# Attention, gated MoE and token/channel mixer on one core: Strassen weight tiles built piece by piece from plain float32 blocks, and second-layer operand sums on VectorE

## The chip, the cores and the metric

One core of a Trainium2 chip runs the whole program. The metric is the device time of one launch in microseconds (us). Five engines take part: PE (TensorE, matrix products), DVE (VectorE), ACT (ScalarE), POOL (GpSimd) and SP (SyncE), which issues every DMA of this kernel in the order in which the DMAs were written to its queue.

## The reference

Three stages follow one another (batch 4, 448 tokens, model width 768).

```python
# attention: 12 heads of 64, q and k normalised first
attn = softmax(scale * rmsnorm(q, g_q) @ rmsnorm(k, g_k).T) @ v
x = attn.transpose(0, 2, 1, 3).reshape(B, S, 768)
# gated unit
h = relu(x @ w_in); u, v = h[..., :512], h[..., 512:]
v_s = w_spatial @ layernorm(v) + b_spatial        # over tokens
x = (u * v_s) @ w_out
# mixer
u = x + (relu(x.T @ w_tok1) @ w_tok2).T           # over tokens
out = u + relu(u @ w_ch1) @ w_ch2                 # over channels, 768 -> 1536 -> 768
```

The weights `w_in`, `w_out`, `w_tok*` and `w_ch*` arrive as 64-bit floats.

## The kernel before, in words

**Planner.** The program is written as generators that yield between small steps. `merge` interleaves several generators; every instruction goes into a `Plan`, which estimates its cost (`estimate`), schedules all of them by a list scheduler (`place`) and then issues each engine's instructions in the planned order. All compute instructions are issued from one line (L418), so rows of the profile are told apart by tile names. An engine works its queue strictly in order, SP too.

**Number format.** Float32 products run as three passes over operands that are split in two parts: `HI` (rounded, written by ACT) and `LO` (the rest, a subtraction on DVE or POOL). `convert` turns 64-bit weights into float32 words: one ACT operation (Abs), two DVE `TENSOR_SCALAR` and two DVE `SCALAR_TENSOR_TENSOR`.

**Stages in time.** Attention runs in 24 slots (`Attention.slot`), two heads each; beside it run the preparation of weights and the gated unit (`moe`) of the first three batches. Then the last batch's `moe` runs beside the first token products. Then come the token products of all batches (`tokens`: tiles `h1ps`, `u_ps`, `tp<-x`), then the first channel layer `up` (tile `h2ps`), then the second one `down` (tile `o_ps`).

**Strassen.** Both channel layers use a Strassen-Winograd scheme with seven products of half-size blocks, in the order A11, A12, S2, S3, S1, S4, A22 (`PRODUCTS`). Each product has an operand made from the data (`operand`, from in-place sums in `sums`) and a weight tile of 128 x 2 x 2304 (HI and LO). The weight of a product is a block (B11, B21, B22) or a combination of blocks (T1 = B12 - B11, T2 = B22 - T1, T3 = B22 - B12, T4 = T2 - B21). A product of `up` is 12 groups of 9 matmuls; one of `down` is 7 groups of 18 matmuls. Weight tiles share two buffers (tag `w`), so the tile of a product can be written only after the product two places before it has ended. Operands have two buffers in `up` and three in `down`.

**Where the weight tiles come from.** All seven of each layer are made ahead of use, split and stored to scratch in device memory (`c1_d`, `c2_d`), and `fetch` reads one back (three DMAs of 768 KB) when its product comes up. The first layer's seven are made during attention by `blocks` (tiles `half`, `part`; 9 rounds of 4 conversions, 4 differences on POOL and 7 splits of 256 columns). Of the second layer, B11 and B21 are made by `plain` beside the last `moe` (tile `part`, 24 conversions and splits of 192 columns), and the other five by `mixed` beside `tokens` and `up` (tiles `s`, `half`, `h`, `part`; 12 conversions and 30 splits of 384 columns).

**Sums of the second layer.** In `down`, the sums for S2 and S3 (two each per slice of 128 columns, 28 in all, rows `c<-c,c 128x768`) run on POOL, in place.

## Time and profile before

| | us |
|---|---|
| median of 3 runs | 960.1 (959.32 to 965.97) |
| the profiled execution | 958.78 |
| its span, first to last instruction | 957.0 |
| PE / DVE / ACT / POOL busy in the span | 888.3 / 694.3 / 542.8 / 507.9 |
| attention with three `moe` | 0 to 480 |
| last `moe` and first token products | 480 to 572 |
| `tokens` | 572 to 650 |
| `up` | 650 to 801 |
| `down` | 801 to 957 |

The stage borders are read from the timeline to within a few us. A busy PE is not PE at its peak, since matmuls are pipelined and the ends of their rows are modelled; how much work a stage holds is read from counts and from stretches in which matmuls of one kind follow one another closely.

### The profile page before, as it was taken

How to read it: one execution, taken by the hardware profiler on the slowest of the kernel's cores; microseconds unless marked ns; L12 is line 12 of the kernel's file. 1: busy time of each engine (PE TensorE's matmuls, PEld its weight loads, DVE VectorE, ACT ScalarE, POOL GpSimd, SP SyncE). 2: the span in 40 equal slices, each digit the busy share in tenths (PEclk: the TensorE clock that was granted, in tenths of full speed). 3: DMA queues.
4: the chain of work that ended last, by engine and by line, in shares of the span. 5: the costliest groups of instructions: out<-in, count | busy, mean ns of one | idle time of the engine just before them, and what ended most of it. 6: DMA issues, size and time to landing. Idle time of an engine off the chain costs nothing.

```text
span 957.0 us, 16041 instructions
## 1 busy us (share of the span) xinstructions
PE 888.3 (93%) x5134; PEld 722.5 (76%) x5134; DVE 694.3 (73%) x1364; ACT 542.8 (57%) x1312; POOL 507.9 (53%) x609
## 2 busy tenths in 40 slices
PE   3888899999998989989989988989999999999998
PEld 1434467677565767657868987879998899999998
DVE  4888889886899787997636744784798754576753
ACT  5998978777767776775635533545423443322221
POOL 2465654786367675566723811465633208984340
PEclk9998999999999999998989999998999999999999
DMA  6655645567746667655588577963787673352461
GB/s 149 162 152 159 175 132 150 157 189 222 222 113 205 200 201 232 200 160 177 184 282 260 207 225 250 330 216 101 248 276 259 241 252 114 133 183 99 148 216 66
DMA packets 166245, 182.99 MB, mean 191 GB/s; under 512 B 77329, under 2 KB 138577, under 8 KB 164625
## 3 DMA queue, kind: packets, MB, share of 16 engines
q1 hardware_dynamic: 166160, 181.96, 60.9%
q8 instruction: 41, 0.67, 0.3%
q14 instruction: 44, 0.35, 0.1%
HBM read 124.24 MB, written 57.67 MB: 190 GB/s over the span
## 4 chain that ended last, share of the span: by engine, by line
PE 44%; DVE 7%; DMA 6%; ACT 3%; issue 3%; POOL 1%; SPq 0%; ACTq 0%; POOLq 0%; DVEq 0%
PE o_ps L418 16%; PE h2ps L418 14%; DMA c_d<-part 4%; PE xps L418 2%; PE u_ps L418 2%; PE tp L418 2%; PE ups L418 2%; PE vps L418 2%; DVE part L418 1%; DVE half L418 1%; PE av L418 1%; PE h1ps L418 1%; PE sps L418 1%; DMA x_d<-xo 1%; DMA x<-x_d 1%
## 5 line engine op out<-in xcount | busy, mean ns | idle before, releaser
L418 PE MATMUL h2ps<-op,w 128*128 128x448 f32 x756 | 157.7, 370 | 4.6 <-DVE x L418 3.3
L418 PEld LDWEIGHTS h2ps<-op,w 128*128 128x128 f32 x756 | 142.9, 190 | 17.7 <-DVE x L418 3.6
L418 PE MATMUL o_ps<-w,op 128*128 128x384 f32 x882 | 153.1, 334 | 0.0
L418 PEld LDWEIGHTS o_ps<-w,op 128*128 128x128 f32 x882 | 152.9, 188 | 0.0
L418 ACT ACTIVATE e<-sc,nm 112x448 f32<-112x448 f32 x192 | 120.5, 637 | 27.2 <-DVE nm L418 14.9
L418 DVE TENSOR_REDUCE nm<-sc 112x1 f32<-112x448 f32 x192 | 110.4, 614 | 13.1 <-PE sc L418 12.4
L418 PE MATMUL tp<-ident,e 112*128 112x112 f32 x672 | 94.3, 264 | 9.3 <-ACT e L418 3.1
L418 PEld LDWEIGHTS tp<-ident,e 112*128 112x128 f32 x672 | 73.1, 142 | 36.1 <-ACT et L418 4.7
L418 ACT ACTIVATE op<-c 128x768 fp32r<-128x768 f32 x49 | 41.6, 848 | 102.7 <-PE o_ps L418 101.4
L418 POOL TENSOR_SCALAR e<-e,sums 112x448 f32<-112x448 f32 x112 | 78.1, 710 | 17.2 <-DVE sums L418 12.7
L418 DVE TENSOR_TENSOR op<-c,op 128x768 fp32r<-128x768 f32 x49 | 68.8, 1405 | 22.7 <-ACT op L418 22.7
L418 PE MATMUL ups<-xp,wu 128*128 128x448 f32 x288 | 71.7, 385 | 5.3 <-ACT e L418 3.2
L418 DVE TENSOR_TENSOR c<-c,h2ps 128x448 f32<-128x448 f32 x84 | 50.6, 617 | 32.9 <-PE h2ps L418 32.8
L418 ACT ACTIVATE et<-tp 128x448 f32<-128x448 f32 x120 | 64.8, 548 | 16.4 <-PE tp L418 14.6
L418 POOL TENSOR_TENSOR c<-c,c 128x768 f32<-128x768 f32 x28 | 58.7, 2119 | 26.1 <-ACT c L418 23.1
L418 PE MATMUL xps<-wo,g 128*128 128x256 f32 x432 | 64.4, 299 | 6.4 <-ACT xo L418 6.2
L418 PE MATMUL av<-et,v 128*64 128x448 f32 x288 | 67.3, 557 | 0.5 <-ACT tg L418 0.5
L418 PEld LDWEIGHTS xps<-wo,g 128*128 128x128 f32 x432 | 57.3, 199 | 11.4 <-ACT xo L418 6.9
L418 PEld LDWEIGHTS ups<-xp,wu 128*128 128x128 f32 x288 | 52.5, 192 | 13.3 <-ACT e L418 3.6
L418 DVE TENSOR_TENSOR part<-half,part 128x256 fp32r<-128x256 f32 (+1 forms) x78 | 45.2, 582 | 18.1 <-ACT part L418 17.9
L418 POOL TENSOR_TENSOR u<-u,o 128x384 f32<-128x384 f32 x28 | 34.7, 1249 | 43.6 <-DVE o L418 30.4
L418 PE MATMUL vps<-wv,xp 128*128 128x512 f32 x216 | 56.9, 408 | 0.0
(136 smaller groups left out, 1797.4 us busy)
## 6 DMA issues: line engine op xcount, KB each, us to landing
w<-c_d SPq DMA_DIRECT2D x42, 768.0 KB, 6.6
c_d<-part SPq DMA_DIRECT2D x63, 256.0 KB, 2.9
wu<-wu_d SPq DMA_DIRECT2D x16, 768.0 KB, 5.2
wo<-wo_d SPq DMA_DIRECT2D x12, 1024.0 KB, 5.3
c_d<-part SPq DMA_DIRECT2D x30, 384.0 KB, 3.1
raw<-in_moe_w_ch_dram SPq DMA_DIRECT2D x36, 256.0 KB, 3.0
raw<-in_q_dram SPq DMA_DIRECT2D x48, 112.0 KB, 3.1
u<-u_d SPq DMA_DIRECT2D x28, 192.0 KB, 4.2
```

Of the source, the lines that this page charges most:

```text
L418: getattr(getattr(self.nc, op.engine), fn)(*args, **kwargs)
```

## The change

Scratch now holds plain float32 blocks without the split: B11, B12, B21, B22 of both layers, and later T1 and T2. Making a block is a conversion and a store alone (`whole`). B11 and B21 of the first layer are converted during attention (18 pieces of 256 columns), its B12 and B22 beside the last `moe` (18 more), and all four of the second layer beside `tokens` and `up` (24 pieces of 384 columns).

`fetch` is replaced by `build`: when a weight tile is due, its 2304 columns are made in six pieces of 384. A piece fetches one to three blocks (tile `src`, six buffers, 192 KB each), takes differences on POOL, splits on ACT and DVE (tile `w`), and for T2 stores T1 and T2 back to scratch. So each of the 14 tiles costs 6 ACT copies and 6 DVE subtractions shortly before its product, and each layer 24 POOL subtractions.

The sums of `down` run on DVE in place of POOL; those of `up` stay on POOL. In the planner the assumed cost of a DMA with long rows changes, and the slot windows of the merged generators change. `divisors` takes its tile from another pool.

```diff
-        return max(475, size / (380 if n >= 512 else 260)), 2400 + 1.2e-3 * size
+        return max(475, size / 260), 2400 + 1.2e-3 * size
...
-    c1_d = [scratch([P, 2, JH * FH], F32R, f"c1_d{n}") for n in range(7)]
-    c2_d = [scratch([P, 2, KH * DH], F32R, f"c2_d{n}") for n in range(7)]
+    B11, B12, B21, B22, T1, T2 = range(6)
+    c1_d = [scratch([P, JH * FH], F32, f"c1_d{n}") for n in range(6)]
+    c2_d = [scratch([P, KH * DH], F32, f"c2_d{n}") for n in range(6)]
...
-            wide = mp.tile([T, 2 * C, D], F32, tag="half0", bufs=1, name="wide")
+            wide = p.tile([T, 2 * C, D], F32, tag="wide", bufs=1, name="wide")
...
+    def whole(pool, src, dst, n, k, w, tags):
+        raw, word = tags
+        r, q = divmod(k, 2)
         cols = src.shape[1] // (2 * W)
+        for i in range(n):
             rows = (r * n + i) * P
+            for c in range(0, cols, w):
+                m = min(w, cols - c)
+                at0 = (q * cols + c) * W
+                x = weights(pool, raw, 2, src[rows:rows + P, at0:at0 + m * W], P, (m,))
+                t = pool.tile([P, m], U32, tag=word, bufs=2, name="word")
+                t = convert(pool, None, 0, x, P, m, None, None, at=t)
+                nc.sync.dma_start(out=dst[k][:, i * cols + c:i * cols + c + m], in_=t)
+                yield
...
+    def build(wp, src, kind):
+        n = src[0].shape[1]
+        t = wp.tile([P, 2, n], F32R, tag="w", bufs=2, name="w")
+        for c in range(0, n, DH):
+            cs = slice(c, c + DH)
+            def fetch(k):
+                x = wp.tile([P, DH], F32, tag="src", bufs=SRC, name="src")
+                nc.sync.dma_start(out=x, in_=src[k][:, cs])
+                return x
+            def less(x, y, k=None):
+                nc.gpsimd.tensor_tensor(x, x, y, op=ALU.subtract)
+                if k is not None:
+                    nc.sync.dma_start(out=src[k][:, cs], in_=x)
+                return x
+            if kind == "T2":
+                b12, b11, b22 = fetch(B12), fetch(B11), fetch(B22)
+                x = less(b22, less(b12, b11, T1), T2)
+            elif kind == "T3":
+                x = less(fetch(B22), fetch(B12))
+            elif kind == "T4":
+                x = less(fetch(T2), fetch(B21))
+            else:
+                x = fetch(kind)
+            nc.scalar.activation(t[:, HI, cs], x, AF.Copy)
+            nc.vector.tensor_tensor(t[:, LO, cs], x, t[:, HI, cs].bitcast(F32), op=ALU.subtract)
+        return t
+    SRC = 6
...
-            nc.gpsimd.tensor_tensor(s(to), s(a), s(b), op=op)
+            on.tensor_tensor(s(to), s(a), s(b), op=op)
...
-            w = fetch(wp, c2_d[k])
+            w = build(wp, c2_d, k)
             for m in range(M):
-                make = sums(hs[0], lambda x, m=m: x[:, :, m * P:(m + 1) * P])[name]
+                make = sums(hs[0], lambda x, m=m: x[:, :, m * P:(m + 1) * P], nc.vector)[name]
...
-        (chain(prepare_next(mp), blocks_ch1(mp)), C + 2 * KT + 7 * 9, UO1 + 0.5, NP),
+        (chain(prepare_next(mp), plain(mp, w_ch1, c1_d, JH, (B11, B21))), C + 2 * KT + 18, UO1 + 0.5, NP - 2),
...
-        (plain_ch2(mp), 4 * KH, 0, 0.9))
+        (plain(mp, w_ch1, c1_d, JH, (B12, B22)), 18, 0, 0.7))
...
-        (mixed_ch2(wp, keep), 6 * KH, 0.1, 0.9))
+        (chain(*(whole(wp, wdram(w_ch2), c2_d, KH, k, DH, ("s", "word")) for k in (B11, B21, B12, B22))),
+         4 * KH, 0.05, 0.8))
```

How the planner now orders the engines is shown at three places, all on DVE. The first is in the second half of attention, between the row maxima of the scores (`nm<-sc`). Before, conversions (`half<-raw`, `half<-half`) and splits (`part`) of the first channel layer stand there:

```order
L418 TENSOR_REDUCE nm<-sc 112x1 x2
L418 TENSOR_TENSOR part<-half,part 128x256
L418 TENSOR_TENSOR part<-part 128x256
L418 COPY et<-tp 128x448
L418 TENSOR_SCALAR half<-half 128x256 x2
L418 SCALAR_TENSOR_TENSOR half<-raw,half 128x256
L418 TENSOR_SCALAR sums<-sums 112x4
L418 TENSOR_TENSOR part<-half,part 128x256
L418 SCALAR_TENSOR_TENSOR half<-raw,half 128x256
L418 TENSOR_TENSOR part<-half,part 128x256
L418 TENSOR_TENSOR xp<-av,xp 128x448
```

In the changed kernel a like place holds conversions (`word`) and no split:

```order
L418 TENSOR_REDUCE nm<-sc 112x1 x4
L418 TENSOR_SCALAR word<-word 128x256 x2
L418 SCALAR_TENSOR_TENSOR word<-raw,word 128x256
L418 COPY et<-tp 128x448
L418 SCALAR_TENSOR_TENSOR word<-raw,word 128x256
L418 TENSOR_SCALAR word<-word 128x256
L418 TENSOR_TENSOR tv<-sps,bb 128x448
L418 SCALAR_TENSOR_TENSOR word<-raw,word 128x256
L418 TENSOR_SCALAR sums<-sums 112x4
L418 RECIPROCAL sums<-sums 112x4
```

The `part` rows are gone from this stage, and half of the conversions stand in a later one.

The second place is in `up`, where product A12 ends and S2 begins. Before, the sums of A12 (`c_8642<-c_8500,h2ps`) are followed at once by those of S2 (`c_8500<-c_8500,h2ps`):

```order
L418 TENSOR_TENSOR part<-half_8523,part 128x384
L418 TENSOR_TENSOR c_8642<-c_8500,h2ps 128x448
L418 TENSOR_SCALAR half_8767<-half_8767 128x384
L418 TENSOR_TENSOR c_8642<-c_8500,h2ps 128x448
L418 TENSOR_TENSOR op<-ut,op 128x1344
L418 TENSOR_TENSOR c_8500<-c_8500,h2ps 128x448 x3
```

Now A12's sums are named `c_8197<-c_8023,h2ps` and S2's `c_8023<-c_8023,h2ps`, and between them stand pieces of the weight tile T2 (`w<-src,w`) for S2 itself:

```order
L418 TENSOR_TENSOR w<-src,w 128x384 x2
L418 TENSOR_TENSOR op<-ut,op 128x1344
L418 TENSOR_TENSOR c_8197<-c_8023,h2ps 128x448 x3
L418 SCALAR_TENSOR_TENSOR word<-raw,word 128x384
L418 TENSOR_TENSOR c_8197<-c_8023,h2ps 128x448 x3
L418 TENSOR_TENSOR w<-src,w 128x384
L418 TENSOR_TENSOR op<-ut,op 128x1344
L418 TENSOR_TENSOR w<-src,w 128x384
L418 TENSOR_SCALAR word<-word 128x384
L418 TENSOR_TENSOR c_8023<-c_8023,h2ps 128x448 x5
```

The fifth and sixth piece of T2 stand behind the last sum of A12, and so does S2's operand (`op<-ut`).

The third place is in `down`, at product S2 (sums `o<-o,o_ps`). Before, operand splits and sums alternate:

```order
L418 TENSOR_TENSOR op<-c_8642,op 128x768
L418 TENSOR_TENSOR o_9780<-o_9780,o_ps 128x384
L418 TENSOR_TENSOR op<-c_8642,op 128x768
L418 TENSOR_TENSOR o_9780<-o_9780,o_ps 128x384
L418 TENSOR_TENSOR op<-c_8642,op 128x768
```

Now the sums of the operands (`c<-c,c`, shape 6 x 128) and pieces of the next weight tile stand between them:

```order
L418 TENSOR_TENSOR o_9502<-o_9502,o_ps 128x384
L418 TENSOR_TENSOR c_8023<-c_8023,c_8197 128x6x128
L418 TENSOR_TENSOR op<-c_8197,op 128x768
L418 TENSOR_TENSOR w<-src,w 128x384 x2
L418 TENSOR_TENSOR o_9502<-o_9502,o_ps 128x384
L418 TENSOR_TENSOR op<-c_8197,op 128x768
L418 TENSOR_TENSOR c_8197<-c_8826,c_8197 128x6x128
L418 TENSOR_TENSOR w<-src,w 128x384
```

Per slice DVE now has up to four kinds of work where it had two; POOL's 28 rows `c<-c,c` are gone from this stage, and 24 rows `src<-src 128x384` stand there.

## Rows read from the trace of the kernel before

**Rows 1.** Busy time by stage (us; A:B, length, engines with instruction counts, clock, DMA)
```profile
130.00:230.00 100.00, 98.75 (x637) 71.98 (x634) 85.38 (x201) 78.11 (x216) 68.88 (x104) 1.00 0.62 172
230.00:480.00 250.00, 232.67 (x1455) 167.81 (x1455) 207.22 (x489) 174.36 (x484) 157.93 (x234) 0.99 0.63 191
480.00:572.00 92.00, 85.52 (x488) 78.23 (x485) 52.13 (x134) 40.92 (x104) 37.37 (x43) 0.94 0.75 243
572.00:650.00 78.00, 68.84 (x386) 63.18 (x385) 52.74 (x81) 36.78 (x69) 32.32 (x25) 0.94 0.79 266
650.00:801.00 151.00, 149.61 (x735) 137.55 (x734) 103.32 (x154) 65.47 (x107) 60.79 (x39) 1.00 0.62 213
801.00:957.00 156.00, 152.57 (x881) 152.25 (x879) 93.02 (x97) 42.73 (x55) 83.67 (x51) 1.00 0.42 145
```
**Rows 2.** Groups on DVE, 230 to 480 us: count, busy us, mean ns, idle before
```profile
L418 DVE SCALAR_TENSOR_TENSOR half<-raw,half 128x256 uint32<-128x256 uint32 x72 | 34.3, 487 | 0.3
L418 DVE TENSOR_TENSOR part<-half,part 128x256 fp32r<-128x256 f32 x54 | 30.1, 559 | 14.0 <-ACT part L418 13.9
...
L418 DVE TENSOR_SCALAR half<-half 128x256 f32<-128x256 f32 x36 | 16.3, 458 | 4.6 <-ACT half L418 4.5
...
L418 DVE TENSOR_SCALAR half<-half 128x256 uint32<-128x256 uint32 x36 | 11.8, 331 | 0.2
```
**Rows 3.** Timeline, attention: start us, length us, engine, what [idle before]
```profile
306.59 3.17 DVE L418 TENSOR_SCALAR half<-half 128x256 f32<-128x256 f32 x1
...
310.35 1.08 PE L418 MATMUL ups<-xp,wu 128*128 128x448 f32 x4 [2.19 <-DVE et L418]
```
**Rows 4.** Waits of ACT, 480 to 572 us: total, times, longest
```profile
ACT part L418 <- DMA c_d<-part: 10.7, 9, 3.9
```
**Rows 5.** Chain that ended last: long runs of matmuls (start us, us)
```profile
651.20 59.60 PE h2ps L418 x294
...
800.66 152.92 PE o_ps L418 x882
```
**Rows 6.** Timeline of DVE in `up`
```profile
706.42 0.55 DVE L418 SCALAR_TENSOR_TENSOR half<-s,half 128x384 uint32<-128x384 uint32 x1
...
707.72 0.35 DVE L418 TENSOR_SCALAR half<-half 128x384 f32<-128x384 f32 x1
...
708.45 0.55 DVE L418 TENSOR_TENSOR part<-half,part 128x384 fp32r<-128x384 f32 x1
709.00 0.62 DVE L418 TENSOR_TENSOR c<-c,h2ps 128x448 f32<-128x448 f32 x1
...
736.02 1.55 DVE L418 TENSOR_TENSOR op<-ut,op 128x1344 fp32r<-128x1344 f32 x1
```
**Rows 7.** Timeline of POOL and DVE in `down`
```profile
825.97 13.81 POOL L418 TENSOR_TENSOR c<-c,c 128x768 f32<-128x768 f32 x6
...
832.80 0.96 DVE L418 TENSOR_TENSOR op<-c,op 128x768 fp32r<-128x768 f32 x1 [0.26 <-ACT op L418]
835.92 2.16 DVE L418 TENSOR_TENSOR op<-c,op 128x768 fp32r<-128x768 f32 x1 [0.26 <-ACT op L418]
```
**Rows 8.** Groups on DVE, 801 to 957 us
```profile
L418 DVE TENSOR_TENSOR op<-c,op 128x768 fp32r<-128x768 f32 x47 | 66.9, 1424 | 22.4 <-ACT op L418 22.4
L418 DVE TENSOR_TENSOR u<-u,o_ps 128x384 f32<-128x384 f32 x28 | 15.5, 553 | 25.1 <-PE o_ps L418 25.1
```
**Rows 9.** Groups on POOL, 570 to 957 us
```profile
L418 POOL TENSOR_TENSOR u<-u,o 128x384 f32<-128x384 f32 x28 | 34.7, 1249 | 43.6 <-DVE o L418 30.4 <-DMA u<-u_d 11.7 <-ACT o L418 1.4
L418 POOL TENSOR_TENSOR ut<-ut 128x1344 f32<-128x1344 f32 x8 | 26.4, 3299 | 14.9 <-ACT ut L418 9.3 <-DVE op L418 5.6
L418 POOL TENSOR_TENSOR half<-half,h 128x384 f32<-128x384 f32 x12 | 12.9, 1071 | 39.7 <-DVE part L418 39.3
```
**Rows 10.** DMA issues by size: count, KB each, median us to landing
```profile
u<-u_d SPq DMA_DIRECT2D x28, 192.0 KB, 4.2
...
c_d<-part SPq DMA_DIRECT2D x24, 192.0 KB, 2.6
```

More of the change, by code (lines that the diff above doesn't have):

```diff
@@ new lines, in plain @@
+    def plain(mp, src, dst, n, ks):
+        for k in ks:
+            yield from whole(mp, wdram(src), dst, n, k, NX, ("wraw", "wpart"))
+    def build(wp, src, kind):
[24 more added lines that the diff above has]
+        return t
@@ L1274, in store, with sums @@
             nc.sync.dma_start(out=u_d[b * S + t:b * S + t + m, :], in_=self.x[b, c][:m])
[L1277 removed]
+    def sums(x, s, on):
         (x11, x12), (x21, x22) = x
         def put(to, a, b, op=ALU.subtract):
[L1283 removed]
+            on.tensor_tensor(s(to), s(a), s(b), op=op)
         def s2():
@@ L1298, in sums @@
         }
-    PRODUCTS = (("A11", B11), ("A12", B21), ("S2", T2), ("S3", T3), ("S1", T1), ("S4", B22), ("A22", T4))
+    PRODUCTS = (("A11", B11), ("A12", B21), ("S2", "T2"), ("S3", "T3"), ("S1", T1), ("S4", B22), ("A22", "T4"))
     def operand(pool, shape, tag, bufs, make):
@@ L1308, in operand @@
         return t
-    def fetch(wp, src):
-        t = wp.tile([P, 2, src.shape[2]], F32R, tag="w", bufs=2, name="w")
-        n = src.shape[2] // JH
-        for j in range(JH):
-            js = slice(j * n, (j + 1) * n)
-            nc.sync.dma_start(out=t[:, :, js].bitcast(F32), in_=src[:, :, js].bitcast(F32))
-        return t
     def up(wp, chan, ut):
@@ L1322, in up @@
             cp.tile([P, KH, SH], F32, tag=f"c{n}", bufs=1, name=f"c{n}") for n in ("11", "12", "21", "22"))
-        first = [sums(((ut[0, 0], ut[0, 1]), (ut[1, 0], ut[1, 1])), lambda x, b=b: x[:, b]) for b in range(B // 2)]
+        first = [sums(((ut[0, 0], ut[0, 1]), (ut[1, 0], ut[1, 1])), lambda x, b=b: x[:, b], nc.gpsimd) for b in range(B // 2)]
         for name, k in PRODUCTS:
-            w = chan.pop(k, None) or fetch(wp, c1_d[k])
+            w = chan.pop(k, None) or build(wp, c1_d, k)
             for b in range(B // 2):
@@ L1488, in before_up @@
         for k in (B11, B21):
-            chan[k] = fetch(wp, c1_d[k])
+            chan[k] = build(wp, c1_d, k)
         yield from tokens()
```

104 lines of the change are left out of this document (removed).

## The prediction

> **What bounds the kernel now.** I read the busy times by stage first [rows 1], then the groups and the timeline of the stages in which TensorE is not full, last the chain of waits. In `up` and `down` PE is the bound: 149.61 of 151 us and 152.57 of 156 us busy [rows 1], and the chain that ended last is one run of 294 `h2ps` matmuls in 59.60 us (0.203 us each) and one of 882 `o_ps` matmuls in 152.92 us (0.173 us each) [rows 5]. Nothing that only relieves another engine there can shorten them. Attention from 230 to 480 us is different: PE is busy for 232.67 of 250 us and DVE for 207.22, its highest share of all stages but the one before, and PE issues 5.8 matmuls per us against 6.4 in the 100 us ahead [rows 1]. Of DVE's 207 us, the conversions and splits of the first channel layer take 34.3 + 30.1 + 16.3 + 11.8 = 92.5 us [rows 2]. That they are in the way is seen in the timeline: one conversion row of 256 columns, 0.46 us on the mean, takes 3.17 us, the evacuation of a transpose behind it on DVE comes late, and PE stands idle for 2.19 us with the releaser DVE `et` [rows 2, 3]. From 480 to 572 PE lacks 6.5 us and from 572 to 650 9.2 us [rows 1]; in the first of these ACT, which works in order, waits 10.7 us in nine waits for stores of finished pieces to free their buffer [rows 4].
>
> **The change part by part.**
>
> *Attention, 230 to 480.* Removed: all splits and the POOL differences, and half of the 36 conversions. A conversion of 256 columns costs DVE 0.458 + 0.331 + 2 x 0.487 = 1.76 us [rows 2], so 18 of them cost 31.7 us where 92.5 stood: 61 us less on DVE, 146 of 250 instead of 207. (Nine more splits, those of T3, are left out of the sum.) PE becomes the bound. At the busy share of the stretch before (98.75 of 100) the 232.67 us of PE work take 235.6 us, 14 less than now; at its rate of 6.37 matmuls per us the 1455 matmuls take 228.4 us, 22 less. I take the middle, **-18**, and 14 to 22 as its bounds for the case that DVE is what held PE; less if it is the dependence from slot to slot (second rival). Stage 0 to 230 keeps its instructions; the planner's order differs in places, for which I allow 4 either way and put in 0.
>
> *Last `moe`, 480 to 572.* 24 conversions with splits of 192 columns give way to 18 conversions of 256 without. Each piece had two ACT copies and now has one, and the stores that ACT waits for go from 24 to 18 here. PE's idle time is 6.5 us; I take **-4** (0 to -8).
>
> *`tokens`, 572 to 650.* New are the twelve pieces of the first two tiles, 12 x 0.55 = 6.6 us on DVE by the 0.55 us row of a 384-column split [rows 6], and earlier conversions; gone are the splits and the POOL work of the second layer. DVE is busy for 52.74 of 78 us [rows 1], which covers it: **0** (4 either way). If that cover fails, the first layer starts later by at most those 6.6 us.
>
> *`up` and `down`: load of DVE.* I counted DVE's instructions in the new order between the sums of one product and the next, and priced them by rows in which DVE was alone: `word` rows 0.55 and 0.35, `w` 0.55, sum from PSUM 0.62 (448 columns) and 0.55 (384), operand split 1.55 in `up` [rows 6, 8] and 0.96 in `down` [rows 7], operand sum 0.96 like the split of its size. In `up` from S3 to A22: 60 sums 37.0, 53 conversion rows 24.1, 24 pieces 13.2, nine operand splits 12.8, five operand sums 4.8, together 92 us, where the same count before gives 62. PE needs 4 x 108 x 0.203 = 87.6 us. In `down` from A11 to S3: 28 splits 26.8, 23 operand sums 22.0, 24 pieces 13.2, 21 sums 11.6, together 73.7 us (before 38.5), against 4 x 126 x 0.173 = 87.4 us of PE. Both: 165.7 of DVE against 175 of PE. The rest of `down` has slack (40 us of DVE against 66).
>
> On top comes waiting behind POOL. Beside `c<-c` rows on POOL an operand split of `down` takes 2.16 us, and 0.96 without [rows 7]; the 47 splits take 66.9 us where 47 x 0.96 = 45 would do [rows 8], 22 us of waiting at 83.67 us of POOL [rows 1], 0.26 us per us. The sums that read PSUM are not stretched: 553 ns mean, like the 0.55 of one alone. In the two stretches above POOL has nine and 18 `src` subtractions of about 1.07 us, one `ut` of 3.3 and seven `u` of 1.25 [rows 9], 41 us. At 0.26 that is 11 us of waiting; DVE's share of rows that can be held up grows from 45 of 156 to about 117 of 175, 2.3 times, which would give 25. So DVE needs 177 to 191 us against 175, and falls behind by 2 to 16. A fall-behind of up to about 8 us costs nothing: with two operand buffers, the split of an operand has half a product, 54 x 0.203 = 10.9 us, less its own 1.55 and ACT's copy before it. Left are 0 to 8; I take **+5** (0 to 24).
>
> The Trainium skill, SBUF — State Buffer, section Who interferes with whom, says more than the rows: a DVE instruction with two SBUF inputs and a POOL instruction that reads SBUF exclude each other for the whole instruction. By that rule all 41 us could be added and the term would be 165.7 + 41 - 175 - 8 = +24; the trace agrees in kind (0.96 against 2.16 in rows 7) but shows about a quarter of POOL's time as DVE's wait.
>
> *`up` and `down`: the tile T2.* A wait is added: a tile's pieces are written when its buffer comes free, one product before its use. T2 takes three fetches, two POOL subtractions and two stores per piece, with `src` buffers for two pieces. In `up` the planner itself puts its last two pieces behind A12's last sum, so PE stands for at least that sum and a piece, 0.62 + 0.55 [rows 6], some 1.5 us with the hops. By the rows a round of two pieces takes 4.2 (a fetch of this size) + 2.14 (two subtractions) + 0.55 (split) + 2.6 (store) = 9.5 us [rows 6, 9, 10]. The first round is ready before the buffer is, two follow: 1.5 + 19 = 20.5 of the 21.9 us that A12 takes. Two us more per round, for the queue of SP, make it 24.5, late by 2.6, and the operand split of S2 stands behind it on DVE. In `down` the pieces are done two groups earlier. I take **+4** (1 to 14). Queued behind a late piece on DVE are S2's operand and the sums that free PSUM; PE waits for both.
>
> *POOL's 28 sums of `down` gone, less traffic.* Worth nothing by themselves: PE shows no idle time in `down`, and DMA is busy for 0.42 of it [rows 1].
>
> **Sum.** -18 - 4 + 0 + 5 + 4 = -13. The profiled execution took 958.78 us (span 957.0, and 1.78 around it): 945.8. It lies 1.3 below the median of the runs, so I say **946**; its own range, by the bounds of the terms, is 937 to 955.
>
> **The rivals.**
> - *Better.* DVE and POOL, relieved in attention, give the upper bound there (22) and 8 beside the last `moe`, and the 8 us of slack hide DVE's load (0, T2 +1): 958.8 - 29 = 930. For: in the stretch 130 to 230 PE reaches 98.75% with DVE at 85%. Against: the planner's order is fixed by estimates, and PE also waits for ACT.
> - *No change.* Either attention is held by the chain score, maximum, exponential, transpose, of which DVE is only one link, and gives 5 instead of 18: 958.8 - 5 - 4 + 9 = 959; or the new load on DVE eats the gain, at +24 by full exclusion: 958.8 - 22 + 24 + 4 = 965. For: in `down` the count per slice doubles. Against: 61 us is a third of DVE's time in that stage.
> - *Slower.* One mechanism: the rounds of T2, behind SP. SP works in order, and between T2's fetches stand stores of `word` pieces that wait for DVE, which is itself late. With a round of r us T2 is late by 1.5 + 2r - 21.9 in `up` and 6.2 less in `down` (two groups of 18 x 0.173). At r = 20 that is 19.6 + 13.4 = 33, with DVE's 5 and the gain of 22: 958.8 + 16 = 975. It eats the gain from r = 16 on; the rows give 9.5, so it needs queueing of 6.5 us a round.
>
> **How the numbers follow.** Forecast 0.46, better 0.16, no change 0.25, slower 0.13. A measurement of this kernel tells about 1% from no change: 950.5 and 969.7. Of the forecast's range 937 to 955 some 85% of the chance lies under 950.5, so faster is 0.39 + 0.16 = 0.55, within 1% is 0.07 + 0.25 = 0.32, slower 0.13. The range reaches down to the better case and up to where the slower one begins: 928 to 968.
>
> **What would show it.** Right: from 230 us on, DVE busy about 60% up to the last score, PE over 95%, and attention ending near 462; `up` longer than 151 us by 3 to 10, with an idle PE at the start of S2 whose releaser is DVE `w`; `down` with short PE gaps in S2 and S3 at most. The operand sums near 1 us when alone. Wrong: attention ending within 5 us of 480; or PE gaps at each product of `down`, or an S2 of `up` that starts more than 10 us late; or DVE rows `w` and `c<-c` of 1.5 us and more on the mean.

## The result and the profile after

The changed kernel takes 911.97 us (median of 4 runs, 911.36 to 912.7) against 962.02 of the kernel before (median of 4 runs, one more than in the table further up): 0.9477 of its time, 95% interval 0.9438 to 0.9516. I had said 946, with 928 as the lower end. The profiled execution took 912.7 us, its span is 910.2.

Busy time by stage, as in [rows 1], with borders at the same places of the program:

```profile
0.00:122.00 122.00, 97.69 (x560) 49.72 (x560) 97.58 (x203) 100.85 (x274) 66.14 (x114) 0.99 0.58 155
122.00:222.00 100.00, 99.83 (x642) 71.95 (x642) 79.72 (x189) 76.83 (x213) 65.41 (x100) 1.00 0.59 168
222.00:450.00 228.00, 226.46 (x1464) 166.38 (x1464) 167.24 (x397) 154.20 (x421) 124.38 (x203) 1.00 0.50 146
450.00:529.00 79.00, 77.46 (x463) 71.33 (x460) 37.56 (x94) 31.00 (x71) 22.73 (x21) 1.00 0.71 229
529.00:597.00 68.00, 65.49 (x396) 63.01 (x396) 47.87 (x84) 37.77 (x73) 24.07 (x16) 0.98 0.71 227
597.00:750.00 153.00, 151.97 (x739) 138.20 (x738) 132.67 (x213) 73.41 (x128) 48.77 (x28) 1.00 0.63 184
750.00:910.00 160.00, 153.99 (x883) 152.60 (x881) 128.42 (x156) 58.26 (x91) 69.98 (x52) 1.00 0.43 135
```

Set beside [rows 1], stage by stage:

| stage | before | after | change | predicted |
|---|---|---|---|---|
| start and first half of attention | 230 | 222 | -8 | 0 |
| second half of attention | 250 | 228 | -22 | -18 |
| last `moe` | 92 | 79 | -13 | -4 |
| `tokens` | 78 | 68 | -10 | 0 |
| `up` and `down` | 307 | 313 | +6 | +9 |

The columns that moved are PE's idle time and its clock. In the last `moe` and `tokens` PE was idle for 6.5 and 9.2 us at a granted clock of 0.94 on the mean; now for 1.5 and 2.5 us at 1.00 and 0.98. The first row of the table, -8, holds the same instructions on both sides by my count; a part of it is clock too, 0.96 in the first 130 us before and 0.99 in the first 122 us now:

```profile
0.00:130.00 130.00, 100.34 (x567) 51.54 (x568) 100.53 (x212) 104.45 (x282) 66.93 (x115) 0.96 0.60 155
```

The clock over the whole span, before and after:

```profile
core 0: 957.0 us, clock 0.980
```
```profile
core 0: 910.2 us, clock 0.996
```

957.0 x 0.020 is 19.1 us lost to the lower clock before, 910.2 x 0.004 is 3.6 after. This is an estimate, since it counts PE as working all the time that the clock is low. By it some 15 of the 47 us are clock that no longer drops. In the kernel before, seven stretches in which the clock is granted at its lower level (1.2 in place of 2.4 GHz) hold nearly all of it. Six of them follow a wait of PE of 2.0 to 4.0 us, the seventh, at 585 us, a row of shorter waits. Two of the seven, and the wait ahead of the first:

```profile
428.00:437.00 9.00, 6.80 (x25) 5.14 (x26) 7.20 (x20) 3.94 (x11) 4.32 (x6) 0.62 0.36 116
490.00:499.00 9.00, 7.02 (x26) 6.16 (x27) 2.34 (x9) 3.25 (x8) 2.06 (x3) 0.62 0.90 288
```
```profile
430.20 3.36 PE L418 MATMUL ups<-xp,wu 128*128 128x448 f32 x8 [3.15 <-ACT e L418]
```

DVE's groups in attention, 222 to 450 us, answering to [rows 2] (count, busy us, mean ns, idle before):

```profile
L418 DVE SCALAR_TENSOR_TENSOR word<-raw,word 128x256 uint32<-128x256 uint32 x48 | 22.0, 467 | 0.5
...
L418 DVE TENSOR_SCALAR word<-word 128x256 uint32<-128x256 uint32 x24 | 10.8, 463 | 0.1
L418 DVE TENSOR_SCALAR word<-word 128x256 f32<-128x256 f32 x24 | 10.2, 437 | 3.6 <-ACT word L418 3.6
```

Where the splits and conversions took 92.5 us there are 43.0 (24 pieces fall in this window, not 18), and DVE is 73% busy.

All waits of PE in `up` and `down` that the trace names (total us, times, longest):

```profile
PE o_ps L418 <- ACT w L418: 1.4, 1, 1.4
PE o_ps L418 <- DVE u L418: 1.2, 1, 1.2
PE h2ps L418 <- DVE c L418: 1.0, 3, 0.5
```

The new work on DVE there, in `up` (first two rows) and in `down` (the rest, beside [rows 8]):

```profile
L418 DVE TENSOR_TENSOR w<-src,w 128x384 fp32r<-128x384 f32 x37 | 27.1, 751 | 1.2 <-ACT w L418 1.2
...
L418 DVE TENSOR_TENSOR op<-ut,op 128x1344 fp32r<-128x1344 f32 x13 | 21.8, 1678 | 1.1 <-ACT op L418 1.1
...
L418 DVE TENSOR_TENSOR op<-c,op 128x768 fp32r<-128x768 f32 x47 | 55.7, 1185 | 9.5 <-ACT op L418 9.3
L418 DVE TENSOR_TENSOR w<-src,w 128x384 fp32r<-128x384 f32 x36 | 27.0, 780 | 2.2 <-ACT w L418 2.2
L418 DVE TENSOR_TENSOR c<-c,c 128x768 f32<-128x768 f32 x23 | 26.6, 1165 | 0.0
```

DVE is 87% busy in `up` and 80% in `down`, and PE waits for it for some 2 us in this order of the program.

Of the waits of [rows 4] nothing is left: in the changed kernel ACT waits for no store of a piece in the last `moe`. What such a wait can do is seen in the chain of waits of that stage, 480 to 572 us of the kernel before:

```profile
by line: DMA c_d<-part 18.2%; PE xps L418 17.5%; PE vps L418 10.2%; PE ups L418 8.0%; PE h1ps L418 6.3%; PE sps L418 6.1%; DVE part L418 5.2%; issue 5.1%; DMA x<-x_d 2.9%; ACT part L418 2.8%; PE av L418 2.5%; DMA x_d<-xo 2.2%; POOL vn L418 
```

The largest single entry of the chain is the landing of finished pieces. One instance in its timeline:

```profile
486.65 0.53 SPq L418 DMA_DIRECT2D c_d<-part  x1
...
488.49 0.84 ACT L418 ACTIVATE xh<-x 128x768 fp32r<-128x768 f32 x1 [1.54 <-DMA x<-x_d]
...
491.20 0.37 ACT L418 ACTIVATE part<-raw 128x192 f32<-128x192 f32 x1 [1.60 <-DMA c_d<-part]
491.54 0.38 ACT L418 ACTIVATE xo<-xps 128x256 f32<-128x256 f32 x1
...
491.98 2.93 PE L418 MATMUL xps<-wo,g 128*128 128x256 f32 x12 [3.98 <-ACT xo L418]
```

A store is issued at 486.65. ACT, which works in order, waits 1.60 us for it to land before it may write the next piece into that buffer; behind the piece stands the evacuation `xo` that frees PE's accumulator. PE stands for 3.98 us in all, in the first part of which ACT waited for a load of `x`; from 491 on PE runs at the lower clock. In the changed kernel the chain of the same stage (450 to 529 us) holds one store of a piece, 4.1% of the stretch:

```profile
475.23 3.22 DMA c_d<-word
```

How much such waits are worth is tried below (s1).

### The profile page after: what moved, and what is told of

Read it like the earlier page. It is cut to its first block, busy times and chain, and to the rows that moved or that the text cites. A ratio compares the mean times of both kernels' runs of the same rounds, so it can differ in the third digit from the quotient of the medians.

```text
span 910.2 us, 15803 instructions
## 1 busy us (share of the span) xinstructions
PE 872.9 (96%) x5134; PEld 713.2 (78%) x5134; DVE 691.1 (76%) x1335; ACT 532.3 (58%) x1267; POOL 421.5 (46%) x533
## 4 chain that ended last, share of the span: by engine, by line
PE 78%; DVE 7%; ACT 6%; DMA 4%; issue 2%; SPq 1%; POOL 1%; ACTq 0%; DVEq 0%; POOLq 0%
PE o_ps L418 15%; PE h2ps L418 15%; PE tp L418 8%; PE av L418 6%; PE ups L418 6%; PE vps L418 6%; PE sc L418 5%; PE xps L418 5%; PE sps L418 4%; ACT e L418 3%; PE u_ps L418 3%; PE h1ps L418 3%; SPq L418 1%; DVE word L418 1%; DMA c_d<-word 1%
## 5 line engine op out<-in xcount | busy, mean ns | idle before, releaser
L418 POOL TENSOR_TENSOR src<-src 128x384 f32<-128x384 f32 x48 | 61.3, 1288 | 102.3 <-DMA src<-c_d 94.8
L418 POOL TENSOR_SCALAR e<-e,sums 112x448 f32<-112x448 f32 x112 | 71.9, 658 | 38.6 <-DVE sums L418 14.5
L418 DVE TENSOR_SCALAR word<-word 128x256 uint32<-128x256 uint32 (+5 forms) x132 | 58.2, 456 | 25.7 <-ACT word L418 24.6
L418 DVE SCALAR_TENSOR_TENSOR word<-raw,word 128x256 uint32<-128x256 uint32 (+2 forms) x132 | 74.1, 567 | 1.1
L418 POOL TENSOR_TENSOR u<-u,o 128x384 f32<-128x384 f32 x28 | 41.1, 1480 | 62.9 <-ACT o L418 34.2
L418 DVE TENSOR_TENSOR op<-c,op 128x768 fp32r<-128x768 f32 x49 | 57.6, 1176 | 9.5 <-ACT op L418 9.3
L418 PE MATMUL xps<-wo,g 128*128 128x256 f32 x432 | 62.2, 290 | 1.2 <-DVE sums L418 0.8
L418 DVE TENSOR_TENSOR w<-src,w 128x384 fp32r<-128x384 f32 x84 | 60.0, 737 | 3.4 <-ACT w L418 3.4
L418 PEld LDWEIGHTS xps<-wo,g 128*128 128x128 f32 x432 | 55.1, 190 | 6.6 <-issue 1.3
```

Source lines behind the costliest of these rows:

```text
L418: getattr(getattr(self.nc, op.engine), fn)(*args, **kwargs)
```

## The experiments

Eighteen kernels. Medians in us; ratios to the kernel before in the same job, with the 95% interval.

| kernel | us | ratio |
|---|---|---|
| d1_dve_back | 932.2 | 0.968 [0.963, 0.973] |
| d2_act_pool_back | 921.0 | 0.957 [0.952, 0.963] |
| w1_before_less_dve | 942.0 | 0.979 [0.975, 0.983] |
| a1_sums_pool | 939.2 | 0.975 [0.971, 0.979] |
| n1_lo_pool | 923.5 | 0.962 [0.957, 0.967] |
| b1_dma_cost | 945.8 | 0.985 [0.979, 0.991] |
| a2_old_dma_cost | 929.1 | 0.967 [0.962, 0.972] |
| p1_before_other_order | 953.6 | 0.993 [0.988, 0.998] |
| p1_after_other_order | 915.4 | 0.954 [0.948, 0.959] |
| p2_after_third_order | 924.8 | 0.960 [0.956, 0.963] |
| h2_layer2_alone | 917.8 | 0.953 [0.948, 0.958] |
| ph2_other_order | 915.9 | 0.954 [0.951, 0.957] |
| s1_stores_unhooked | 949.8 | 0.988 [0.985, 0.991] |
| m1_before_no_ch2_pieces | 936.5 | 0.976 [0.973, 0.979] |
| m2_layer2_plus_old_pieces | 948.0 | 0.987 [0.984, 0.991] |
| m3_old_pieces_dma_only | 939.2 | 0.975 [0.967, 0.983] |
| m4_old_pieces_compute_only | 924.4 | 0.961 [0.953, 0.968] |
| m5_old_pieces_small_dma | 931.9 | 0.966 [0.961, 0.970] |

**How far the order alone moves the time.** The planner orders all instructions anew after any edit. Three kernels change nothing but a constant of its matmul cost:

```diff
-                return 0.326 * n if ins[0].shape[0] <= 64 else n / 2.4 + 13, 200
+                return 0.326 * n if ins[0].shape[0] <= 64 else n / 2.4 + 14, 200
```

(12 in the third order of the changed kernel.)

> The kernel before with one constant of the planner's matmul cost 1 ns higher (13 to 14): the same instructions, another order. If the order alone scatters the time by as much as the runs so far suggest (before and its copy with the new DMA cost lie 14 us apart, the change and its copy with the old one 17 us), 945 to 975; if the order matters little, within 4 us of before.

> The changed kernel with the same planner constant 1 ns higher. If the order scatters, 912 to 935, 912 being a lucky draw; if not, 910 to 916.

> The changed kernel with one constant of the planner's matmul cost moved by 1 ns the other way: a third order of the same instructions. 905 to 925, by the scatter of the orders run so far; under 911 it would be a faster version than the changed kernel.

Orders of the kernel before: 960 and 954. Of the changed kernel: 912, 915 and 925, mean 917. A difference of less than about 13 us between two single kernels therefore names no cause, and the pair at hand, 50 us apart, lies about 10 above the difference of the means, 957 and 917. None of the orders beats 912. The order moves even the part that no edit touches: the 192nd of the 384 `av` matmuls, halfway through attention and about where the first layer's pieces begin or before it, starts between 219 and 237 us in the kernels of the table below.

**Is DVE's load in attention what held PE?** d1 puts 144 DVE instructions without use (60 us, in bunches of eight) into the changed kernel's attention, d2 puts 63 ACT copies and 36 POOL subtractions there, w1 takes two of four conversion steps and the `LO` splits (65 us of DVE) out of the attention of the kernel before.

```diff
+                    for _ in range(8):
+                        d = pool.tile([P, m], U32, tag="dummy", bufs=1, name="dummy")
+                        nc.vector.scalar_tensor_tensor(
+                            d, t.bitcast(U32), 29, t.bitcast(U32), ALU.logical_shift_right, ALU.bitwise_or)
```
```diff
+                    for n_ in range(3 + (i + c // w) % 2):
+                        d = pool.tile([P, m], F32, tag="dummy", bufs=1, name="dummy")
+                        nc.scalar.activation(d, t, AF.Copy)
+                        if n_ < 2:
+                            nc.gpsimd.tensor_tensor(d, d, t, op=ALU.subtract)
```
```diff
-            nc.vector.scalar_tensor_tensor(a, high, 0xC0000000, a, ALU.bitwise_and, ALU.bitwise_or)
-            nc.vector.scalar_tensor_tensor(a, low, 29, a, ALU.logical_shift_right, ALU.bitwise_or)
...
-            nc.vector.tensor_tensor(t[:, LO], x, t[:, HI].bitcast(F32), op=ALU.subtract)
```

> The changed kernel with 144 additional DVE instructions in attention (eight per converted piece of B11 and B21, 0.42 us each alone, 60 us in all, results unused), so that DVE there has again the load that the change took away, but ACT, POOL and the stores have not. Theory A, DVE's load is what held TensorE from 230 us on, and the idle time also cost clock: the last av matmul goes back from 450 us to 470 or later, half-clock stretches return, the time is 930 to 950. Rival B, the gain came from fewer ACT copies, POOL differences and stores, or from another order in the planner: below 920.

> The changed kernel with 63 additional ACT copies (0.42 us) and 36 POOL subtractions (0.73 us) of 256 columns in attention, results unused: the load of ACT and POOL that the change took away, with DVE relieved. Theory A: TensorE is not held, 910 to 920. Rival B: 930 or more.

> The kernel before without two of the four DVE steps of each conversion and without the LO subtraction of the first layer's tiles in attention (leaves these out; both halves of the tiles get HI): about 65 us less on DVE, ACT, POOL and stored bytes as before. Theory A, DVE's load holds TensorE in attention: last av at 455 to 468 instead of 481, 935 to 948. Rival: within 5 us of before in attention.

932, 921 and 942: 20 and 9 us lost against 912, 18 gained on 960. d2's 9 us lie within the scatter of the orders. Of d1's 20, 13 to 18 stand in attention (the last `av` at 468.2, against 450 to 455 in the three orders of the changed kernel), so added DVE load costs PE time there, 0.2 to 0.3 us per us of DVE. w1 ends attention at 473.3, 8 us before the kernel before and later than I had named. b1 below ends it as early (472.8) with all of DVE's work, and w1 also stores each piece in two halves, so w1 shows nothing for DVE by itself. And h2 below shows that the real instructions, put back in their real place, cost much less than d1's.

**The parts of the change.** a1 leaves the sums of `down` on POOL, n1 moves the `LO` split of unsummed tiles to POOL; b1 gives the kernel before the planner's new DMA cost alone, and a2 the changed kernel the old one.

```diff
-                make = sums(hs[0], lambda x, m=m: x[:, :, m * P:(m + 1) * P], nc.vector)[name]
+                make = sums(hs[0], lambda x, m=m: x[:, :, m * P:(m + 1) * P], nc.gpsimd)[name]
```
```diff
-            nc.vector.tensor_tensor(t[:, LO, cs], x, t[:, HI, cs].bitcast(F32), op=ALU.subtract)
+            on = nc.vector if isinstance(kind, str) else nc.gpsimd
+            on.tensor_tensor(t[:, LO, cs], x, t[:, HI, cs].bitcast(F32), op=ALU.subtract)
```
```diff
-        return max(475, size / (380 if n >= 512 else 260)), 2400 + 1.2e-3 * size
+        return max(475, size / 260), 2400 + 1.2e-3 * size
```

> The changed kernel with the sums of the second layer on POOL again. By the prediction's step DVE is overfull from S2 to S3 of down: with 28 sums less (27 us alone) the gaps in down (154.0 busy, some 4 us of gaps) go, 906 to 911. Rival, the sums on DVE are what makes down work beside the builds, since POOL now also has 24 subtractions: POOL needs about 2 x 1.83 + 1 us per slice of 3.1 us in S2 and S3, PE waits there, 915 to 930.

> The changed kernel with the LO part of the eight tiles that are plain blocks or T1 (48 pieces) made on POOL instead of DVE. DVE loses 48 x 0.55 = 26 us in up and down, POOL gets 48 us. If DVE's load is what leaves gaps in up and down (about 5 us more than pure matmul time), 905 to 909; if the exclusion of DVE and POOL decides, 912 to 920.

> The kernel before with the planner's new cost for DMAs with long rows alone; nothing else changes but the order. Theory A: within 1% of before, 953 to 970. Rival, the order itself gives much of the gain (the change is 4 to 7 us early already at 100 us, where it issues the same instructions): below 945.

> The changed kernel with the planner's old cost for DMAs: 905 to 920 by theory A; above 925 if the new cost is what made the gain.

a1 takes 939, 27 more, beyond both ranges that I had named. Only part of that is the sums: `down`, from its first to its last matmul, takes 170.1 us against 154.9 to 156.4 in the three orders of the changed kernel, and the other 12 us stand ahead of `up`, where a1 has the changed kernel's instructions in another order. In `down`, with the subtractions for the weight tiles already on POOL, the sums make the operands late, and PE waits for them where it had waited for nothing of the kind; the clock there is 0.97 on the mean:

```profile
PE o_ps L418 <- ACT op L418: 5.9, 1, 5.9
PE o_ps L418 <- DVE op L418: 5.1, 4, 2.1
```

So beside the builds the sums on DVE are worth some 14 us; what the move would do without the builds was not run. n1 is 11 slower than the changed kernel, outside both of its ranges but within the scatter: its loss stands ahead of `up`, and its `down`, 154.8, is as long as the others'. The planner's DMA cost is worth 14 us on the kernel before (b1, between its two ranges) and 17 in the changed one (a2; 12 against the mean of the three orders). Both have the same sign, but each is a single order and hardly clear of the scatter; how the dearer DMA helps was not tried.

**The second layer alone.** h2 has the first layer as before (all seven tiles made in attention by `blocks`, read back whole) and the second layer, its sums and the planner's cost as after; ph2 is another order of it.

```diff
-            w = chan.pop(k, None) or build(wp, c1_d, k)
+            w = chan.pop(k, None) or fetch_old(wp, c1_d[O[ONAME[name]]])
...
-        (chain(prepare_next(mp), plain(mp, w_ch1, c1_d, JH, (B11, B21))), C + 2 * KT + 18, UO1 + 0.5, NP - 2),
+        (chain(prepare_next(mp), blocks_ch1(mp)), C + 2 * KT + 7 * 9, UO1 + 0.5, NP),
...
-        (plain(mp, w_ch1, c1_d, JH, (B12, B22)), 18, 0, 0.7))
```

> Layer 1 as before (seven tiles made in attention, read back), layer 2 as in the change (plain blocks, build, sums on DVE). Theory A: attention is as slow as before (last av at 475 to 485), only the last moe, which loses its 24 conversions, and the clock there get better: 940 to 955. Rival, most of the gain comes from the second layer or from the planner: below 930.

> The kernel h2_layer2_alone with one constant of the planner's matmul cost moved by 1 ns, which gives another order of the same instructions: measures how far the order alone moves this kernel. 912 to 930 if the order's scatter is what the pairs of before (960, 954) and of after (912, 915) show; a time over 935 would say that h2_layer2_alone's 918 was luck.

918 and 916, as fast as the changed kernel's three orders, though all 63 splits of the first layer and the other half of its conversions are made again before `up`, 49 of the 63 in attention and 14 beside the last `moe`. DVE is busy for 83% of attention in h2, as in the kernel before, and PE for 97%:

```profile
222.00:463.00 241.00, 234.51 (x1497) 170.01 (x1497) 198.99 (x469) 174.19 (x480) 160.36 (x236) 1.00 0.60 181
```

So the relief of attention, my largest term, is not where the time came from. Read from the traces, as the starts of matmuls, in us (`av` ends attention, `xps` the last `moe`; `h2ps` is `up`, `o_ps` is `down`):

| kernel | 192nd `av` | last `av` | last `xps` | first `h2ps` | last `h2ps` | last `o_ps` |
|---|---|---|---|---|---|---|
| before | 225.4 | 481.5 | 571.6 | 637.8 | 800.3 | 953.2 |
| p1 (before) | 232.2 | 481.9 | 562.9 | 634.4 | 792.1 | 945.0 |
| b1 | 232.6 | 472.8 | 556.5 | 627.0 | 786.9 | 939.8 |
| w1 | 231.9 | 473.3 | 555.5 | 627.1 | 783.4 | 936.4 |
| s1 | 229.1 | 480.0 | 570.8 | 634.1 | 791.4 | 944.3 |
| after | 219.0 | 450.1 | 528.9 | 588.8 | 749.8 | 906.4 |
| p1 (after) | 222.7 | 455.2 | 537.8 | 594.3 | 753.7 | 909.6 |
| p2 (after) | 222.1 | 453.8 | 531.7 | 592.4 | 762.9 | 918.0 |
| a1 | 228.4 | 462.7 | 540.0 | 600.3 | 762.8 | 933.1 |
| n1 | 222.5 | 455.3 | 537.9 | 598.7 | 762.5 | 917.5 |
| a2 | 223.8 | 460.1 | 539.6 | 599.8 | 766.6 | 920.4 |
| d1 | 226.6 | 468.2 | 547.4 | 606.6 | 770.3 | 926.0 |
| d2 | 221.3 | 457.7 | 537.8 | 596.6 | 765.3 | 922.9 |
| h2 | 224.9 | 463.2 | 540.0 | 599.4 | 756.1 | 910.4 |
| ph2 | 226.3 | 460.1 | 537.7 | 597.2 | 753.9 | 908.0 |
| m1 | 230.2 | 466.9 | 555.6 | 616.9 | 776.8 | 929.7 |
| m2 | 237.1 | 478.6 | 572.2 | 634.4 | 788.8 | 942.6 |
| m3 | 231.8 | 480.1 | 561.5 | 626.0 | 780.8 | 935.0 |
| m4 | 226.2 | 465.6 | 549.5 | 608.8 | 763.2 | 916.8 |
| m5 | 227.8 | 471.3 | 550.9 | 618.2 | 772.4 | 926.2 |

Over their orders, the changed kernel ends attention 9 us before h2 (453.0 against 461.7), and from the first `h2ps` to the last `o_ps` it takes 9 us more (319.5 on the mean of 317.6, 315.3, 325.6, against 311.0 and 310.8). What the first layer gains in attention it gives back in `up` and `down`. Even the gain is no larger than what an order does: a1, with the changed kernel's attention, ends it at 462.7.

**The 24 pieces beside the last `moe`.** What h2 still lacks is `plain_ch2`, 24 loads, conversions, splits and stores of 192 columns. s1 lets their stores read a resident tile, so that no buffer waits for a store; m1 leaves the pieces out of the kernel before; m2 puts them back into h2; m3, m4 and m5 put back only parts of them.

```diff
-            nc.sync.dma_start(out=dst[k][:, :, at0:at0 + w].bitcast(F32), in_=t.bitcast(F32))
+            nc.sync.dma_start(out=dst[k][:, :, at0:at0 + w].bitcast(F32), in_=moe_w["wv"][:, :, 0, :w].bitcast(F32))
```
```diff
-        for i in range(KH):
-            for c in range(0, DH, NX // 2 * 3 // 2):
-                yield from plain(mp, wdram(w_ch2), c2_d, KH, i, c, NX // 2 * 3 // 2, ("wraw", "wpart"))
+        for k in (B11, B21):
+            nc.sync.dma_start(
+                out=c2_d[k].rearrange("p a (f d) -> p a f d", f=KH).bitcast(F32),
+                in_=moe_w["wv"][:, :, :, :DH].bitcast(F32))
+            yield
```
```diff
-        (first_tokens(), 2 + C + 8, 0, 1))
+        (first_tokens(), 2 + C + 8, 0, 1),
+        (plain_ch2(mp), 4 * KH, 0, 0.9))
```

m3, against m2; m5 is m3 with `w // 6` words a row loaded and stored:

```diff
-            t = pool.tile([P, 2, w], F32R, tag=part, bufs=2, name="part")
-            convert(pool, None, 0, x, P, w, t[:, HI], t[:, LO], at=t[:, LO].bitcast(U32))
...
-            nc.sync.dma_start(out=dst[k][:, :, at0:at0 + w].bitcast(F32), in_=t.bitcast(F32))
+            nc.sync.dma_start(
+                out=dst[k][:, :, at0:at0 + w].bitcast(U32), in_=x.rearrange("p (a b) -> p a b", a=2))
```

m4, against m2:

```diff
-            x = weights(pool, raw, 2, src[rows:rows + P, c * W:(c + w) * W], P, (w,))
+            x = moe_w["wv"][:, HI].rearrange("p a b -> p (a b)")[:, :w * W].bitcast(U32)
...
-            nc.sync.dma_start(out=dst[k][:, :, at0:at0 + w].bitcast(F32), in_=t.bitcast(F32))
```

> The kernel before with the 24 stores beside the last moe reading a resident tile instead of the finished piece (the second layer's B11 and B21 get other numbers): the same work and bytes, but no piece's buffer waits for a store. If ACT, standing in its queue before such a buffer, is what holds TensorE beside the last moe, the stretch from the last av to the last xps matmul falls from 90 us to 80 to 85; if not, it stays at 88 or more.

> The kernel before without plain_ch2's 24 pieces (the second layer's plain float32 blocks that run beside the last moe): layer 2's B11 and B21 tiles hold a resident tile's numbers, set by two stores; nothing is changed in attention. Theory (the string of pieces through the two-deep rings is what PE pays for, since the products' pools open only when the last piece is done): the work before the first h2ps falls by far more than the last moe's own 11 us: first h2ps at 600 to 612 instead of 637.8, time 915 to 930. Rival (attention's VectorE load alone): attention and the up product stay within the scatter of the order, the last moe gains 4 to 8, time 944 to 957.

> The kernel h2_layer2_alone (first layer as before, second layer as after) with the 24 old pieces of plain_ch2 put back beside the last moe; what they make goes to scratch that nothing reads. Theory of the string of pieces: last av back at 472 or later, last xps back at 555 or later, time 935 to 950. Rival: attention stays at 463 to 468 and only the last moe pays, time 918 to 926.

> m2_layer2_plus_old_pieces (948) with the 24 pieces cut to their DMAs: each loads its 192 KB and stores the same bytes again; the conversions (ACT, VectorE) and the subtraction (POOL) are left out. If the transfers and the two-deep ring of loads are what costs the 30 us, the time stays at 938 to 950; if the engines' work does, it falls to 914 to 926.

> m2_layer2_plus_old_pieces with the 24 pieces cut to their engine work: two ACT, four VectorE and one POOL instructions each on a resident tile, no load and no store. The mirror of m3_old_pieces_dma_only: 938 to 950 if the engines' work costs the 30 us, 914 to 926 if the transfers do; both in between if the two share it.

> m3_old_pieces_dma_only (939) with the same 24 loads and 24 stores, each cut from 192 KB to 16 KB; the other bytes are left out. If the number of transfers in SP's ordered queue costs the 21 us, the time stays at 932 to 944; if their bytes or the time until they land do, it falls to 914 to 926 (h2_layer2_alone and its other order took 918 and 916).

s1 takes 949.8, 11 less than the kernel before and 4 less than that kernel's other order. Its stretch from the last `av` to the last `xps` stays at 90.8 us, against 90.1 before: by the expectation, the waits for stores are not what holds PE beside the last `moe`. ACT waits less for them there (480 to 571 us), but it waits for the pieces' loads instead:

```profile
ACT part L418 <- DMA raw<-in_moe_w_ch_dram: 11.9, 8, 5.0
...
ACT part L418 <- DMA c_d<-part: 4.5, 4, 2.4
```

The other order of the kernel before says the same. With all its pieces and stores the stretch takes 81.0 us, though ACT waits for stores there (482 to 563 us) no less than in [rows 4]:

```profile
ACT part L418 <- DMA c_d<-part: 12.7, 10, 3.3
```

So the wait at 491 us shows one way in which a piece stops PE, and not the price of the pieces.

m1 gains 24 us (936.5 against 960.8), m2 loses 30 to 32 (948.0 against 917.8 and 915.9). m1's time lies outside what either theory had named, but the rival, 4 to 8 us in the last `moe` alone, is refuted twice. The stretch that goes with the pieces is the one from the last `av` to the first `h2ps`, the last `moe` and `tokens` together: 152 to 156 us in the six kernels that have them whole (before, p1, b1, w1, s1, m2), 136 to 143 in the ten without (the changed kernel, its orders and its variants, h2, ph2), on the mean 16 us apart. m1 lies between, at 150.0; there `mixed` still makes the second layer's other tiles beside `tokens`.

In attention the two tests do not agree. m1 ends `av` 15 us before the kernel before, all of it gained after the 192nd `av`. m2 ends it 15 to 19 us after h2 and ph2, but 11 to 12 of these stand already at the 192nd `av`, when the first piece has only just begun (on ACT at 235.1 us), and belong to the order. So some 20 of m2's 30 us are the pieces'. The last `moe` of h2, then of m2, from the last `av` to the last `xps`:

```profile
463.00:540.00 77.00, 77.00 (x466) 71.56 (x461) 36.67 (x84) 33.19 (x79) 29.93 (x29) 1.00 0.79 253
```
```profile
479.00:572.00 93.00, 84.07 (x473) 77.42 (x472) 50.14 (x134) 39.09 (x103) 37.10 (x42) 0.94 0.73 232
```

PE is never idle in the one; in the other it is for 8.9 us, and the clock is at 0.94. ACT's waits for stores of pieces in these two windows, h2 first:

```profile
ACT part L418 <- DMA c_d<-part: 1.3, 4, 0.5
```
```profile
ACT part L418 <- DMA c_d<-part: 14.2, 8, 4.5
```

Transfers alone (m3) bring 21 of the 30 us back, engine work alone (m4) 7, which is within the scatter. In the stretch from the last `av` to the first `h2ps`, which the order moves less, m2 takes 20 us more than h2, m3 10, m4 7 and m5 11. So both kinds of work cost time there, and cutting the transfers to a twelfth of their bytes (m5 against m3) saves none of it. In m3 ACT and DVE do nothing for the pieces, but SP's queue stands between 440 and 600 us for their landings, 27.7 us in 21 waits:

```profile
SPq L418 <- DMA raw<-in_moe_w_ch_dram: 14.3, 12, 3.6
SPq L418 <- DMA c_d<-raw: 13.4, 9, 3.5
```

In the kernel before it stands for the work on `part` tiles instead (those of the 24 pieces and, up to 477 us, of the first layer's), and everything issued later, `xo` stores and the loads of `x`, `wu` and `wo` among it, stands behind:

```profile
SPq L418 <- DVE part L418: 27.6, 20, 3.5
SPq L418 <- POOL part L418: 13.6, 13, 3.0
...
SPq L418 <- ACT part L418: 5.9, 13, 1.7
```

Those are 47 of 160 us; in the changed kernel SP waits for `word` pieces there for 18 us. But this is no price either: added up over all that it waits for, SP's queue stands for 96 of these 160 us in the kernel before, 100 in m2, 104 in h2 and 106 in the changed kernel. What counts is what stands behind the waiting transfer, and no run isolates that. Over the whole program m5 takes 932, 7 us less than m3 and within the scatter of it, so how the count of transfers and their size share the cost stays open.

The pieces also move the first layer's 63 pieces. ACT's copy for the last of them, in m2 and then in h2:

```profile
471.83 0.42 ACT L418 ACTIVATE part<-half 128x256 fp32r<-128x256 f32 x1 [0.43 <-DMA c_d<-part]
```
```profile
533.03 0.42 ACT L418 ACTIVATE part<-half 128x256 fp32r<-128x256 f32 x1 [0.46 <-DMA c_d<-part]
```

With the first copy at 238.1 and 246.8, the same 63 pieces take 234 us in m2 and 286 in h2 (241 before, 296 in m1). Both layers' pieces use the same two buffers, and where 24 more have to follow, the first 63 are packed a fifth closer into attention. What PE pays for this was not tried alone: after the 192nd `av`, attention takes 3 to 8 us more in m2 than in h2 and ph2, and 13 to 19 less in m1 than in the two orders of the kernel before.

## Why the prediction was wrong

The direction was right, the size by 34 us not. Step by step:

*Attention, -18.* The stage gained 22, so the number looked right, but its reason is not what the runs show. I reasoned that 61 us less on DVE makes PE the bound there. DVE load that is added does cost (d1), but with the first layer's work put back (h2, ph2) DVE is as busy as before, PE is busy for 97%, and attention ends only 9 us later, which another order alone can do (a1). The row that I took as the sign of DVE's load [rows 3] says something else: it ran from 306.59 to 309.76, and POOL worked without a pause beside it, from this row on to 309.61:

```profile
306.63 0.64 POOL L418 TENSOR_SCALAR e<-e,sums 112x448 f32<-112x448 f32 x1
...
308.48 1.13 POOL L418 TENSOR_TENSOR tg<-tg,tv 128x448 f32<-128x448 f32 x1
```

So it is a row stretched beside POOL, like those of [rows 7], and no queue of DVE's own work. A stage's gain that fits is no proof of its mechanism.

*Last `moe`, -4, and `tokens`, 0: the step that failed.* I bounded what the 24 pieces cost by PE's idle time of 6.5 us in the one stage, let 0 stand for the other, where PE was idle for 9.2, and gave them no price anywhere else. In these two stages together the kernels with the pieces take 16 us longer than those without; over the whole program, leaving them out gained 24 us (m1) and putting them back lost 30 (m2, of which 11 to 12 belong to the order). Predicted -4, measured some -20 to -24. Two things went wrong. The clock of 0.94 stood in [rows 1] and I priced only idle time: 170 us x 0.06 = 10 us were to be had from the clock in these two stages, by an estimate from these rows. And I took the waits that I saw beside the pieces for their whole cost. By which wait they hold PE stays open: ACT's waits for stores [rows 4] do not decide it (s1), and of the 20 us in these two stages transfers alone bring 10 and engine work alone 7 (m3, m4).

*Order, 0 (4 either way).* Two orders of one kernel differ by 2 to 13 us, and one constant of the planner's DMA cost, which stands in the diff and which I gave no term, by 12 to 17.

*DVE in `up` and `down`, +5, and T2, +4.* With +6 in the stages' table and +9 against h2, right in sum. What I described is not what one order shows: in the profiled one S2 of `up` starts without a wait for `w`, and PE waits for 1.0 us there. In another (p2, `up` 10 us longer) the longest wait comes from ACT, which stands 6.84 us for the store of a `word` piece, with the copy that frees PE's accumulator behind it. The next falls on sums that stand behind two builds on DVE:

```profile
608.24 0.54 ACT L418 ACTIVATE word<-raw 128x384 f32<-128x384 f32 x1 [6.84 <-DMA c_d<-word]
609.26 26.91 PE L418 MATMUL h2ps<-op,w 128*128 128x448 f32 x117 [4.80 <-ACT c L418]
...
641.65 3.91 DVE L418 TENSOR_TENSOR w<-src,w 128x384 fp32r<-128x384 f32 x2
...
648.48 21.88 PE L418 MATMUL h2ps<-op,w 128*128 128x448 f32 x99 [3.40 <-DVE c L418]
```

So the order decides what shows in `up`. My prices of DVE's rows missed both ways. The `w` rows and operand splits of `up` take 0.75 and 1.68 us on the mean, where I had 0.55 and 1.55. Rows in a run overlap: four sums take 2.20 us, where four times the 0.62 of one [rows 6] are 2.48, 12% less:

```profile
737.49 2.20 DVE L418 TENSOR_TENSOR c<-c,h2ps 128x448 f32<-128x448 f32 x4
```

*Waiting behind POOL, 0.26 us per us.* In `down` after the change: 47 x (1.185 - 0.96) + 36 x (0.780 - 0.55) + 23 x (1.165 - 0.96) = 23.6 us against 70.0 us of POOL, 0.34 us per us. The Trainium skill, SBUF — State Buffer, section Who interferes with whom, calls the ports that the two engines share an exclusive lock; I took that to make DVE's wait the whole of POOL's time, and the rival that rested on this did not come. The trace agrees with a lock and not with my reading of it: the split of 0.96 us at 832.80 [rows 7], which I took for one without POOL, stands beside a row of POOL too, and there POOL's row is the stretched one, 2.62 us. Beside the split of 2.16 us at 835.92 POOL's row takes 1.84:

```profile
832.84 2.62 POOL L418 TENSOR_TENSOR c<-c,c 128x768 f32<-128x768 f32 x1
835.42 1.84 POOL L418 TENSOR_TENSOR c<-c,c 128x768 f32<-128x768 f32 x1
```

In both pairs the row that starts second is the longer one of its kind, so DVE bears only a part of the waiting.

*POOL's sums, 0.* Not tried by itself. Left on POOL beside the builds, which I had not considered, they make `down` some 14 us longer (a1).

*The range and the signs.* The bounds of the terms, added end to end, give 922 to 991; the 937 to 955 that I called the range by these bounds are narrower, without a reason. Of the signs, PE over 95% came (99%); DVE was busy for 73% and not 60%, attention ended at 450 and not near 462, and `up` grew by 2 us, with no wait for `w` at S2.

*The sum by what was measured.* Second-layer pieces -20 to -24, the planner's DMA cost about -13, the first layer -9 and +9: -33 to -37, against -40 between the means of the orders (957 and 917). Each part comes from one or two orders and is no surer than their scatter. The other 10 us of this pair are its order.

*The rivals.* "Better" named 930 by an upper bound in attention and 8 beside the last `moe`: the right side, the wrong place. None of the others occurred.

## What to carry to other kernels

Do not bound the cost of a string of side work by the idle time beside it: 24 small pieces cost some 20 us while PE showed 6.5 us of idle time in their stage. Leaving the string out, or putting it back, prices it; the wait of one engine or queue that stands for it does not, as s1 and the sums of SP's waits show. Read the clock column with the idle column: here the lower clock came behind PE's waits. And where a planner orders everything anew, time two or three orders of each kernel before a difference of a per cent is given a cause, and ask at which point of the program the difference begins: 11 to 12 us of what the 24 pieces seemed to cost stood there when the first piece began.
